# GpSimd's product of a decode chunk one half step after VectorE's join, and the transposes of a three-tile block one step on

## The chip, the cores and the metric

One core of a Trainium2 chip runs the kernel. The time is the device time of one execution in microseconds (us); three runs of the kernel before gave 1037.73 us in the median (1034.54 to 1038.38). TensorE multiplies, VectorE (DVE), ScalarE (ACT) and GpSimd (POOL) do the elementwise work, SyncE (SP) issues most DMAs. Each engine works through its own queue in order.

## The reference, cut to what matters

```python
# attention over packed keys, 4 x 8 heads, 576 tokens, head_dim 64  -> x, 2304 x 512
logits = x @ w_gate + log1p(exp(x @ w_noise)) * noise          # 8 experts
top2   = the two largest of 8, weights by softmax
for e in range(8):                                             # expert layer
    h = maximum(x[mask_e] @ w1[e], 0)                          # 512 -> 1024
    out[mask_e] += weight * (h @ w2[e])                        # 1024 -> 512
g = x @ w_gate2; val = x @ w_val                               # gated layer, 512 -> 1536
return (silu(g) * val) @ w_out                                 # 1536 -> 512
```

The three matrices of the gated layer come in as 64-bit numbers (`wx`), so the kernel has to turn them into pairs of 32-bit parts before it can multiply with them. That is the decode.

## The kernel before

Every product in full precision is made of three matmuls, high by high, high by low and low by high (`mm3`, L628 to L630), in which a value is split into a rounded part and its remainder. The program has three stretches: attention and routing (to about 160 us), the expert layer (to about 605 us) and the gated layer (to the end). The change lies in the expert layer.

**The expert steps.** The expert layer runs over 14 blocks. A block is one expert with three tiles of 128 tokens, or with two: (0,·,3), (1,·,3), then a three-tile and a two-tile block for each of the experts 2 to 5, then (6,·,3), (7,·,3), (6,·,2), (7,·,2). A block has eight steps f = 0 to 7. TensorE does in step f: the up product of f (L628 to L630 on `xTh`, `xTl`), the down product of f - 1 (on `hh`, `hl`), and transposes for the next block where there are any. ScalarE makes `hh` from the up product (L664), VectorE makes `hl` (L665). So `hh` of step f is needed one step later. With three tiles the down products hold three of the eight PSUM banks for the whole block; the up product, the transposes and the decode take turns in the other five.

**What else is issued in a step, in this order.** First `loader.turn()`: it copies a piece of the next expert's weights from `stg` (ACT L148), subtracts for the remainder (L149; on VectorE for a piece of w1, on GpSimd for a piece of w2), and SP issues the load of a later piece (L142). A turn falls in steps 1, 3, 5, 7 of most blocks, but in all eight of the block of expert 1. Then `prep`: one step of `prep_expert` for the next block. Its first steps gather a row tile each (GpSimd's indirect DMA, L623), its later ones transpose a tile each (PE L610, ACT L611, DVE L612). The list `PREP` says in which f the generator takes a step; for a next block of three tiles these are six, three gathers and three transposes. Last the decode: two half steps in a step of a three-tile block (none in f = 0 from expert 2 on), one in a step of a two-tile block.

**The decode.** There are 72 chunks of 128 x 256 numbers. Chunk m is loaded (SP, L763, tile `wd`), masked into exponent and mantissa (`exps`, DVE L771 and L772, tiles `ex` and `mt`), made to floats in a PSUM bank (`floats`, ACT L778 and L779), joined (DVE L785 and L787, which frees the bank), and multiplied on GpSimd (L795). For an odd chunk of the first two matrices GpSimd then makes four sums and differences (L801), and for every odd chunk ScalarE makes the high part (`high`, L818), VectorE the low part (`low`, L824), and SP stores it (`store`, L829). Counted in half steps of the generator, chunk m has its load in 2m, `exps` in 2m + 4, `floats` in 2m + 7, join and product in 2m + 9, `high` in 2m + 11, `low` in 2m + 12 and `store` in 2m + 13. `wd` has five buffers, `ex` and `mt` three each, a pair's `sums` two. The generator has 156 half steps; the blocks up to the last one take exactly 156, and the last block first runs the generator to its end (L1170), before it closes the decode's buffers and opens those of the gated layer's weights in their place.

Of the kernel before, what the change touches and what calls it, by code (L numbers as in the profile page):

```python
# [11 lines left out]
F32 = mybir.dt.float32  # L12
# [3 lines left out]
I32 = mybir.dt.int32  # L16
# [83 lines left out]
def body(ctx, tc, qT, kT, v, pT, noise, wgn, w1, w2, wx, out):  # L100
# [31 lines left out]
    def bank():  # L132
        return psum.tile([128, 512], F32, name="bank", tag="bank")
# [610 lines left out]
    for x in PLAN.split():  # L744
        x, _, n = x.partition("*")
# [4 lines left out]
    dp = wB[2]  # L750
# [5 lines left out]
    def decode():  # L756

        st, sums, his = {}, {}, {}

        def load(n):  # L760
            i, c = divmod(n, 4)
            w = dp.tile([128, 256, 2], I32, name="wd", bufs=5)
            nc.sync.dma_start(w, wx[i, :, c * 256:(c + 1) * 256].bitcast(I32).rearrange("p (n two) -> p n two", two=2))  # L763
            st[n] = [w]

        def exps(n):
            w = st[n][0]
            ex = dp.tile([128, 256], I32, name="ex")
            mt = dp.tile([128, 256], I32, name="mt")
            st[n] += [ex, mt]  # L770
            ve.tensor_scalar(ex, w[:, :, 1], 0x7FF00000, None, op0=ALU.bitwise_and)  # L771
            ve.tensor_scalar(mt, w[:, :, 1], 0xFFFFF, None, op0=ALU.bitwise_and)  # L772

        def floats(n):
            w, ex, mt = st[n]
            fl = bank()
            st[n].append(fl)
            nc.scalar.activation(fl[:, :256].bitcast(I32), ex, AF.Relu, bias=nb896, scale=8.0)  # L778
            nc.scalar.activation(fl[:, 256:], mt, AF.Copy, bias=1.0, scale=2.0 ** -20)  # L779

        def join(n):
            w, ex, mt, fl = st.pop(n)
            i, c = divmod(n, 4)
            mf = mt.bitcast(F32)
            ve.scalar_tensor_tensor(ex, w[:, :, 1], -(1 << 31), fl[:, :256].bitcast(I32), op0=ALU.bitwise_and,  # L785
                                    op1=ALU.bitwise_or)
            ve.scalar_tensor_tensor(mf, w[:, :, 0].bitcast(U32), 2.0 ** -52, fl[:, 256:], op0=ALU.mult, op1=ALU.add)  # L787
            if c % 2 == 0:
                sums[i, c // 2] = dp.tile([128, 8, 128], F32, name="sums", bufs=2)
            q = sums[i, c // 2]  # L790
            if i % 3 == 2:
                o = q[:, 2 * (c % 2):2 * (c % 2) + 2]
            else:
                o = q[:, 4:7:2] if c % 2 else q[:, 0::7]
            nc.gpsimd.tensor_tensor(o, mf.rearrange("p (f n) -> p f n", f=2),  # L795
                                    ex.bitcast(F32).rearrange("p (f n) -> p f n", f=2), op=ALU.mult)
            if c % 2 and i % 3 < 2:

                for o, x, y, op in ((2, 7, 6, ALU.add), (3, 0, 7, ALU.subtract), (1, 2, 0, ALU.subtract),
                                    (5, 4, 1, ALU.subtract)):  # L800
                    nc.gpsimd.tensor_tensor(q[:, o], q[:, x], q[:, y], op=op)  # L801

        def place(n, x):
            i, c = divmod(n, 4)
            p, m = divmod(i, 3)
            o = wq[2 * p + m][:, x, c // 2] if m < 2 else wxo[p][:, x, c // 2 * 512:c // 2 * 512 + 512]
            return o.bitcast(F32)

        def pair(n):

            i, c = divmod(n, 4)
            return sums[i, c // 2], 7 if i % 3 < 2 else 4

        def high(n):
            if n % 2:
                q, k = pair(n)
                h = his[n] = dp.tile([128, 7, 128], F32R, name="his", bufs=1)
                nc.scalar.copy(h[:, :k], q[:, :k])  # L818
                nc.scalar.dma_start(place(n, 0), h[:, :k].bitcast(F32).rearrange("p s n -> p (s n)"))

        def low(n):
            if n % 2:
                q, k = pair(n)
                ve.tensor_tensor(q[:, :k], q[:, :k], his.pop(n)[:, :k].bitcast(F32), op=ALU.subtract)  # L824

        def store(n):
            if n % 2:
                q, k = pair(n)
                nc.sync.dma_start(place(n, 1), q[:, :k].rearrange("p s n -> p (s n)"))  # L829

        N = 72
        for n in range(N + 6):
            for half in (((0, load), (2, exps), (6, low)), ((4, join), (6, store), (5, high), (3, floats))):
                for d, fn in half:
                    if 0 <= n - d < N:
                        fn(n - d)
                yield
# [307 lines left out]
    def xp_acc(i):  # L1145
# [8 lines left out]
    PREP = {2: [1, 0, 1, 0, 0, 1, 1, 0], 3: [1, 1, 1, 1, 1, 1, 0, 0]}  # L1154
    prep0 = prep_pair(0, slot0, FIRST_PLAN)

    blocks = [(0, 2, 3), (1, 2, 3)] + [b for e in range(2, E - 2) for b in ((e, 0, 3), (e, 3, 2))]
    blocks += [(E - 2, 0, 3), (E - 1, 0, 3), (E - 2, 3, 2), (E - 1, 3, 2)]
    dec_g = decode()
    stream = Stream()  # L1160
    rws = ExitStack()
    for i, blk in enumerate(blocks):
# [11 lines left out]
        for f in range(8):  # L1174
# [5 lines left out]
            if f in {4: (1, 2, 4, 5, 7), 3: (0, 1, 2, 3)}.get(left, range(8) if e == 1 else (1, 3, 5, 7)):  # L1180
                loader.turn()
            if [1, 1, 0, 0, 1, 1, 0, 0][f] if left == 2 else PREP[blocks[i + 1][2]][f] if left > 1 else 0:
                next(prep, None)
# [171 lines left out]
```

## Time and profile before

| | |
|---|---|
| median of three runs | 1037.73 us |
| the profiled execution | 1037.31 us |
| its span, first to last instruction | 1035.5 us |
| mean granted clock of TensorE | 0.982 |
| busy: PE, DVE, ACT, POOL | 978.0, 678.6, 421.5, 355.5 us |

A span is the time between the first and the last instruction of the program; the time of the run lies 1.8 us above it. A wait in the profile is the idle time of an engine ahead of an instruction, put down to what ended it. The granted clock is 1.00 where TensorE ran at 2.4 GHz and 0.5 where it ran at 1.2 GHz, averaged over a stretch.

### The profile page before, as it was taken

The numbers are of one execution on the slowest core, as the hardware profiler recorded it, in microseconds if no ns is written. First come the engines' busy times: TensorE is split into PE (matmuls) and PEld (weight loads), VectorE is DVE, ScalarE is ACT, GpSimd is POOL, SyncE is SP. The second block draws the span as 40 slices with busy tenths as digits, with TensorE's granted clock in tenths as the row PEclk, the third lists the DMA queues.
The fourth block names the chain that finished last, engine by engine and source line by source line (L and its number), as shares of the span: only waits on it lengthen the run. The fifth ranks groups of instructions, "written<-read, shape, count | busy, mean of one in ns | idle before, by whom it ended". The sixth has DMA issues, their size and how long they took to land.

```text
span 1035.5 us, 15235 instructions
## 1 busy us (share of the span) xinstructions
PE 978.0 (94%) x5415; PEld 864.9 (84%) x5415; DVE 678.6 (66%) x1536; ACT 421.5 (41%) x859; POOL 355.5 (34%) x409
## 2 busy tenths in 40 slices
PE   6967799989999899998999999999999999999996
PEld 3534689979888798998988898999999999999995
DVE  5998973466565646555645475678865678756764
ACT  2665253465455545555544434222423224132220
POOL 1333532344643545445454414321232211111100
PEclk9978999999999999999999999999999999999999
DMA  8934543377675767666764679887798768777741
GB/s 288 299 122 146 170 136 116 126 273 269 212 264 191 270 204 251 229 202 245 246 225 159 194 210 311 238 236 214 217 303 235 230 184 255 234 199 222 216 147 65
DMA packets 99045, 221.41 MB, mean 214 GB/s; under 512 B 8080, under 2 KB 37392, under 8 KB 96656
## 3 DMA queue, kind: packets, MB, share of 16 engines
q0 software_dynamic: 46752, 104.87, 34.9%
q1 hardware_dynamic: 47024, 101.32, 28.9%
q10 hardware_dynamic: 5184, 14.16, 3.6%
q8 instruction: 45, 0.74, 0.3%
q14 instruction: 40, 0.33, 0.1%
HBM read 172.08 MB, written 48.23 MB: 213 GB/s over the span
## 4 chain that ended last, share of the span: by engine, by line
PE 74%; DVE 10%; DMA 5%; POOL 3%; issue 3%; ACT 3%; SPq 0%; ACTq 0%; POOLq 0%; DVEq 0%
PE bank L628 23%; PE bank L630 23%; PE bank L629 23%; DMA row<-x_dram,idx 3%; POOL sums L801 1%; DMA stg<-in_w 1%; PE bank L610 1%; PE bank L388 1%; POOL w L149 1%; DVE p L460 1%; DVE sums L824 1%; PE bank L919 1%; ACT w L148 1%; POOL sums L795 1%; DMA kt<-in_kT 1%
## 5 line engine op out<-in xcount | busy, mean ns | idle before, releaser
L628 PE MATMUL bank<-w 128*128 128x384 f32 x504 | 170.4, 338 | 0.6 <-ACT hh L993 0.5
L630 PE MATMUL bank<-w 128*128 128x384 f32 x504 | 168.7, 335 | 0.0
L629 PE MATMUL bank<-w 128*128 128x384 f32 x504 | 168.6, 334 | 0.0
L628 PE MATMUL bank<-xTh,w 128*128 128x256 f32 (+1 forms) x512 | 163.1, 319 | 2.8 <-DVE mt L787 2.8
L630 PE MATMUL bank<-xTh,w 128*128 128x256 f32 (+1 forms) x512 | 159.9, 312 | 0.0
L629 PE MATMUL bank<-xTl,w 128*128 128x256 f32 (+1 forms) x512 | 159.7, 312 | 0.0
L665 DVE SCALAR_TENSOR_TENSOR hl<-bank,hh 128x384 fp32r<-128x384 f32 (+1 forms) x128 | 62.4, 488 | 132.3 <-ACT hh L664 125.8
L871 POOL DMA_DIRECT2D w<-wq x72 | 54.4, 756 | 266.3 <-PE bank L630 266.3
L628 PE MATMUL bank<-w,hh 128*128 128x512 f32 x320 | 127.0, 397 | 6.1 <-ACT hh L664 6.1
L630 PE MATMUL bank<-w,hl 128*128 128x512 f32 x320 | 127.4, 398 | 2.8 <-DVE hl L665 2.8
L629 PE MATMUL bank<-w,hh 128*128 128x512 f32 x320 | 127.1, 397 | 0.0
L795 POOL TENSOR_TENSOR sums<-mt,ex 128x256 f32<-128x256 f32 x72 | 54.4, 755 | 170.4 <-DVE mt L787 163.8
L149 POOL TENSOR_TENSOR w<-stg,w 128x1024 fp32r<-128x1024 f32 x37 | 91.4, 2475 | 62.3 <-ACT w L148 62.0
L628 PEld LDWEIGHTS bank<-xTh,w 128*128 128x128 f32 x512 | 98.2, 192 | 7.8 <-DVE mt L787 3.5
L629 PEld LDWEIGHTS bank<-xTl,w 128*128 128x128 f32 x512 | 98.3, 192 | 3.5
L664 ACT ACTIVATE hh<-bank 128x384 fp32r<-128x384 f32 (+1 forms) x128 | 55.5, 433 | 111.5 <-PE bank L630 103.1
L630 PEld LDWEIGHTS bank<-xTh,w 128*128 128x128 f32 x512 | 98.2, 192 | 0.0
L628 PEld LDWEIGHTS bank<-w 128*128 128x128 f32 x504 | 94.6, 188 | 3.1 <-ACT hh L993 1.1
L629 PEld LDWEIGHTS bank<-w 128*128 128x128 f32 x504 | 94.7, 188 | 0.7
L630 PEld LDWEIGHTS bank<-w 128*128 128x128 f32 x504 | 94.6, 188 | 0.0
L630 PE MATMUL bank<-w,lg 128*128 128x512 f32 x204 | 79.7, 391 | 0.0
L629 PE MATMUL bank<-w,hg 128*128 128x512 f32 x204 | 79.7, 390 | 0.0
(222 smaller groups left out, 1838.4 us busy)
## 6 DMA issues: line engine op xcount, KB each, us to landing
w<-wq POOLq DMA_DIRECT2D x36, 1024.0 KB
stg<-in_w SPq DMA_DIRECT2D x64, 512.0 KB
w<-wq POOLq DMA_DIRECT2D x36, 768.0 KB
wd<-in_wx SPq DMA_DIRECT2D x72, 256.0 KB
w<-wxo POOLq DMA_DIRECT2D x18, 1024.0 KB
wq<-his ACTq DMA_DIRECT2D x24, 448.0 KB
wq<-sums SPq DMA_DIRECT2D x24, 448.0 KB
y_dram<-row SPq DMA_DIRECT2D x40, 256.0 KB
```

The source lines that it names most:

```text
L148: nc.scalar.copy(hi, st)
L149: lo_eng.tensor_tensor(lo, st, hi.bitcast(F32), op=ALU.subtract)
L388: nc.tensor.matmul(PS["o", t, c][:n, :272], E2T[t][:, c * 128:c * 128 + n], PP[t], start=True, stop=True)
L460: el.scalar_tensor_tensor(p, p, c[k], x, op0=ALU.add, op1=ALU.mult)
L610: nc.tensor.transpose(ps[:, k, :n], src[:n, k * 128:(k + 1) * 128], ident[:n, :n])
L628: nc.tensor.matmul(ps, lh, rh, start=start, stop=False, skip_group_check=skip)
L629: nc.tensor.matmul(ps, lh, rl, start=False, stop=False, skip_group_check=skip)
L630: nc.tensor.matmul(ps, ll, rh, start=False, stop=stop, skip_group_check=skip)
L664: nc.scalar.activation(hh[:, :n], ps[:, :n], AF.Relu)
L665: ve.scalar_tensor_tensor(hl[:, :n], ps[:, :n], 0.0, hh[:, :n].bitcast(F32), op0=ALU.max, op1=ALU.subtract)
L795: nc.gpsimd.tensor_tensor(o, mf.rearrange("p (f n) -> p f n", f=2), ex.bitcast(F32).rearrange("p (f n) -> p f n", f=2), op=ALU.mult)
L871: nc.gpsimd.dma_start(w[:, :4 * m].rearrange("p (x n) -> p x n", x=4), src.rearrange("p h k n -> p (h k) n"))
```

## The change

The product and GpSimd's sums leave `join` and become a function of their own, `times`, which is issued in the half step after the join. `high`, `low` and `store` move on by one half step each, the load by one half step too, and the order within the half steps changes: the first half step of a round now issues `times`, `exps`, `store`, `high`, the second one `join`, `load`, `low`, `floats`. Chunk m then has its load in 2m + 1, `exps` in 2m + 4, `floats` in 2m + 7, the join in 2m + 9, the product in 2m + 10, `high` in 2m + 12, `low` in 2m + 13, `store` in 2m + 14. The generator has 158 half steps. `wd` has four buffers, `ex` and `mt` four each, which is the same memory. Apart from that, the transposes for a next block of three tiles are made in the steps 4, 5, 6 instead of 3, 4, 5; its gathers stay in 0, 1, 2.

```diff
-            w = dp.tile([128, 256, 2], I32, name="wd", bufs=5)
+            w = dp.tile([128, 256, 2], I32, name="wd", bufs=4)
...
-            ex = dp.tile([128, 256], I32, name="ex")
-            mt = dp.tile([128, 256], I32, name="mt")
+            ex = dp.tile([128, 256], I32, name="ex", bufs=4)
+            mt = dp.tile([128, 256], I32, name="mt", bufs=4)
...
         def join(n):
-            w, ex, mt, fl = st.pop(n)
-            i, c = divmod(n, 4)
+            w, ex, mt, fl = st[n]
             mf = mt.bitcast(F32)
             ve.scalar_tensor_tensor(ex, w[:, :, 1], -(1 << 31), fl[:, :256].bitcast(I32), op0=ALU.bitwise_and,
                                     op1=ALU.bitwise_or)
             ve.scalar_tensor_tensor(mf, w[:, :, 0].bitcast(U32), 2.0 ** -52, fl[:, 256:], op0=ALU.mult, op1=ALU.add)
+
+        def times(n):
+            w, ex, mt, fl = st.pop(n)
+            i, c = divmod(n, 4)
+            mf = mt.bitcast(F32)
             if c % 2 == 0:
                 sums[i, c // 2] = dp.tile([128, 8, 128], F32, name="sums", bufs=2)
...
-        for n in range(N + 6):
-            for half in (((0, load), (2, exps), (6, low)), ((4, join), (6, store), (5, high), (3, floats))):
+        for n in range(N + 7):
+            for half in (((5, times), (2, exps), (7, store), (6, high)), ((4, join), (0, load), (6, low), (3, floats))):
...
-    PREP = {2: [1, 0, 1, 0, 0, 1, 1, 0], 3: [1, 1, 1, 1, 1, 1, 0, 0]}
+    PREP = {2: [1, 0, 1, 0, 0, 1, 1, 0], 3: [1, 1, 1, 0, 1, 1, 1, 0]}
```

## Rows read from the trace of the kernel before

**Rows 1.** The page: the chain that ended last, shares by engine.
```profile
PE 74%; DVE 10%; DMA 5%; POOL 3%; issue 3%; ACT 3%; SPq 0%; ACTq 0%; POOLq 0%; DVEq 0%
```
**Rows 2.** Windows of the expert layer: length, busy (count) by engine, clock, DMA.
```profile
205.00:620.00 415.00, 397.62 (x2220) 356.89 (x2219) 241.56 (x510) 208.62 (x391) 196.85 (x227) 0.99 0.67 228
...
220.00:240.00 20.00, 17.59 (x84) 15.96 (x83) 15.45 (x29) 11.19 (x19) 9.49 (x10) 0.91 0.75 258
```
**Rows 3.** Waits from 205 to 620 us: waiter <- releaser: total us, times, longest.
```profile
POOL sums L795 <- DVE mt L787: 133.2, 41, 6.5
...
ACT his L818 <- POOL sums L801: 31.3, 13, 4.9
...
ACT w L148 <- DMA stg<-in_w: 21.9, 12, 4.5
...
DVE ex L771 <- POOL sums L795: 12.8, 9, 2.9
...
PE bank L610 <- DMA row<-x_dram,idx: 8.3, 4, 2.8
...
PE bank L628 <- ACT hh L664: 6.1, 6, 2.5
...
PE bank L628 <- DVE mt L787: 2.8, 2, 2.4
...
DVE ex L771 <- DMA wd<-in_wx: 2.5, 1, 2.5
```
**Rows 4.** Timeline (start, us, engine, line): first up matmuls of neighbouring steps.
```profile
233.04 0.33 PE L628 MATMUL bank<-xTh,w 128*128 128x384 f32 x1
...
237.23 0.33 PE L628 MATMUL bank<-xTh,w 128*128 128x384 f32 x1
...
278.83 0.28 PE L628 MATMUL bank<-xTh,w 128*128 128x256 f32 x1
...
281.64 0.28 PE L628 MATMUL bank<-xTh,w 128*128 128x256 f32 x1
```
**Rows 5.** Timeline of POOL in the two-tile block of expert 2.
```profile
271.89 2.81 POOL L801 TENSOR_TENSOR sums<-sums 128x128 f32<-128x128 f32 x4
...
279.33 3.00 POOL L149 TENSOR_TENSOR w<-stg,w 128x1024 fp32r<-128x1024 f32 x1 [2.80 <-ACT w L148]
```
**Rows 6.** Timeline of POOL in the two-tile block of expert 3.
```profile
337.86 0.74 POOL L795 TENSOR_TENSOR sums<-mt,ex 128x256 f32<-128x256 f32 x1 [5.93 <-DVE mt L787]
338.68 1.95 POOL L801 TENSOR_TENSOR sums<-sums 128x128 f32<-128x128 f32 x4
340.84 0.98 POOL L623 DMA_INDIRECT row<-x_dram,idx  x1 [0.22 <-PE bank L630]
...
344.43 0.96 POOL L623 DMA_INDIRECT row<-x_dram,idx  x1 [0.16 <-issue]
```
**Rows 7.** Timeline of PE in the same block: transposes that waited.
```profile
347.81 0.63 PE L610 MATMUL bank<-ident,row 128*128 128x128 f32 x4 [2.81 <-DMA row<-x_dram,idx]
```
**Rows 8.** Timeline of ACT ahead of the two-tile block of expert 2.
```profile
274.73 0.94 ACT L818 CAST his<-sums 128x896 fp32r<-128x896 f32 x1 [3.60 <-POOL sums L801]
...
276.91 0.37 ACT L664 ACTIVATE hh<-bank 128x256 fp32r<-128x256 f32 x1
```
**Rows 9.** Timeline of DVE: `low` and then the join, in expert 1's block.
```profile
220.82 1.08 DVE L824 TENSOR_TENSOR sums<-sums,his 128x896 f32<-128x896 f32 x1
...
222.15 0.41 DVE L787 SCALAR_TENSOR_TENSOR mt<-wd,bank 128x256 f32<-128x256 uint32 x1
```
**Rows 10.** Timeline of DVE: a `low` beside POOL's L149 of rows 5.
```profile
278.98 1.08 DVE L824 TENSOR_TENSOR sums<-sums,his 128x896 f32<-128x896 f32 x1
```
**Rows 11.** The page's groups: POOL's subtraction, busy, mean ns of one, idle before.
```profile
L149 POOL TENSOR_TENSOR w<-stg,w 128x1024 fp32r<-128x1024 f32 x37 | 91.4, 2475 | 62.3 <-ACT w L148 62.0 <-issue 0.2
```
**Rows 12.** Waits of SP's queue from 200 to 600 us.
```profile
SPq L763 <- DVE mt L787: 76.7, 30, 6.6
```

## The prediction

> **What bounds the kernel now.** I read the shares of the chain that ended last first: TensorE holds 74% of it [rows 1], so only what makes TensorE wait is worth anything. Then the stretch that the change touches. From 205 to 620 us TensorE is busy for 397.62 of 415 us, so it idles 17.4 us [rows 2]; all 17.4 is the most that shorter waits can give back, but for the clock. The granted clock is 0.91 in two windows of 20 us there, the one shown and the one from 460 us, and 1.00 in the others [rows 2]: 0.09 x 20 = 1.8 us lost in each, both times right behind a long wait. The ceiling is 17.4 + 3.6 = 21.0 us. The waits view says which instructions end the idle time: transposes wait 8.3 us in four places for gathered rows, down products 6.1 us in six places for ScalarE's `hh`, up products 2.8 us in two for a bank that the join frees [rows 3]. Last the timelines around these, for what stood ahead in each queue. A step takes 237.23 - 233.04 = 4.19 us with three tiles and 281.64 - 278.83 = 2.81 us with two [rows 4]; these are the units in which the change moves work.
>
> **Part 1, the transposes.** All four waits for rows lie in the two-tile blocks of experts 2 to 5, where the three-tile block of the next expert is prepared. Expert 3's shows the longest: the first gather starts at 340.84 and its transposes at 347.81, 6.97 us later and after a wait of 2.81 [rows 6, 7]; the other three are of this kind and no longer [rows 3]. One step on is 2.81 us too, so with the gathers where they are now the late tile is in time, by a hair. The next tile decides. In expert 3's block TensorE would have reached its transposes at 347.81 - 2.81 = 345.0; two steps and one set of transposes (some 0.45 us) later, at 351.1, it comes to the second tile, whose gather starts at 344.43 [rows 6] and lands by 344.43 + 6.97 = 351.4. That is 0.3 us late at worst.
>
> The gathers also start earlier. In f = 0 the program issues the gather ahead of the decode. Today the product of the half step before stands in front of it on GpSimd, waiting 5.93 us for the join, and its sums take until 340.6 [rows 6]. With the change that product is behind the gather. The gather of f = 1 gains little: product, sums and a subtraction of 2.48 us still stand ahead of it. I leave 1.0 us of these waits standing, and count the clock dip behind the longest one as gone: 8.3 + 1.8 - 1.0 = **9.1 us**. Bounds: 4.5 us, if the gathers start half a two-tile step (1.4 us) later than now, and 10.1 us.
>
> What the move costs: the third tile is transposed in f = 6, with one step instead of two before the next block's first up product. Its copies need about 0.6 and 0.7 us, the rest of f = 7 covers them. No up product waits for `xTl` on the matmul queue today [rows 3]. I take 0; without the cover it is rival C.
>
> **Part 2, the product.** GpSimd waits 133.2 us for joins, ScalarE's `high` waits 31.3 us in 13 places for GpSimd's sums, and VectorE's masks 12.8 us in nine for products that still read `ex` [rows 3]. These waits are coupled: ScalarE's `high` is held for 3.60 us, until GpSimd's last sum at 274.7, and the `hh` behind it comes two us later, for which TensorE then waits [rows 5, 8]. After the change `high` stands one half step later, which in a three-tile block is a whole step of 4.19 us, while the product can still run right after its join. 13 waits of 31.3 / 13 = 2.4 us, 4.9 at most, mostly end. The fourth buffer of `ex` and `mt` gives the masks two half steps behind the product instead of one: the 12.8 us go as well, though VectorE has room and I count them 0.
>
> What is late next: where GpSimd's subtraction of a weight piece comes in the same step as an odd chunk's product, the product now stands behind it, and the subtraction waits for ScalarE's copy. Counted through the loops, this coincidence occurs in nine steps before and in six after, and three of the six are in expert 1's block, where a turn falls in every step and ScalarE's copies wait for the loads (part of the 21.9 us in rows 3). There subtraction, product and sums take 2.48 + 0.75 + 2.0 = 5.2 us after the copy [rows 6, 11], 1.0 us more than the step that `high` was given.
>
> In expert 1's block the join also moves ahead of `low`. Today `low` runs from 220.82 and the join ends at 222.56 [rows 9]; TensorE's longest wait for a bank ends there. That bank is free up to 1.08 us sooner, but the first transposes still take a bank that leaves the up product behind them with the last join's, so the wait shrinks and does not end. Waits for `hh` and banks with the second dip are 6.1 + 2.8 + 1.8 = 10.7 us. About 4.9 of it lie in expert 1's block (the 2.4, the dip, and one short `hh` wait); I keep 3.0 there. Of the other 5.8 I keep 1.8, for expert 7's block, where ScalarE waits up to 4.5 us for a load of weights [rows 3] whatever GpSimd does. That recovers 10.7 - 4.8 = **5.9 us**. Bounds: -6 us (the product behind subtractions and gathers in all six steps, 1.0 us each) and 10.7.
>
> One row speaks against half of it: a subtraction on GpSimd beside a `low` took 3.00 us, where the mean is 2.475 [rows 5, 10, 11]: `low` ended at 280.06, 0.73 us after that subtraction began. `low` now follows the join directly, so it meets the product which the join releases, for each of the 36 odd chunks. The Trainium skill, SBUF — State Buffer, section "SBUF: two separate sides", says that VectorE and GpSimd share a pair of ports as an exclusive lock, held for a whole instruction. The trace agrees, by these 0.5 us. By that rule the product starts up to 1.08 us after the join, takes back what the reordering gave it, and the forecast would be about 1 us longer.
>
> **Part 3, loads, buffers, tail.** The load comes a half step later and waits for the join of its own half step, as a fifth buffer is gone. SP already waits 76.7 us for joins here [rows 12]. Masks wait for a chunk's arrival once today, 2.5 us [rows 3]; a half step less is 2.81 us in a two-tile block, VectorE can hide that up to once a step, so the load costs between 0 and a few us. I take 0; what stands behind it on SP is rival D. The two extra half steps fall ahead of the last block and hold only the last `store`. If the gathers and loads that reuse the decode's buffers wait for it, this costs up to one step, 2.8 us; I take 0, since VectorE's `low` before it has only moved by one step. New waits that I can't place (0 to 5 us) I set against the intervals between matmuls that are too short for the waits view and shrink with the rest (some 3 us).
>
> **The sum.** 9.1 + 5.9 = 15.0 us, taken from the profiled execution's 1037.31 us (0.4 us under the median of the runs shown): 1022.3, so **1022 us**. Its own range, with 5 us for the new waits and 5 for what I left standing, is 1017 to 1027.
>
> **The rivals.**
> A, the forecast: 58%.
> B, only the transposes gain. The product's waits move into the queue behind subtractions and come back as `hh` waits. For it: the idle time of rows 11 ahead of the subtraction, 62 us on ScalarE's copies. Against it: in two-tile blocks the new order has no such coincidence at all. 1037.3 - 9.1 = 1028, 17%.
> C, given back at block starts. Seven blocks are prepared with the third tile in f = 6; if ScalarE's queue, with a copy of 1 us and `high` of 0.94 us in front, brings `xTl` 2 us late, that is 7 x 2 = 14 us back and the time 1036. Against it: in f = 6 there is mostly no turn, where f = 5 had one. 14%.
> D, slower: SP is held by the joins, so pieces of weights are loaded later. Twelve copies on ScalarE wait for their load already, 21.9 us together [rows 3]. Later by one two-tile step each they would hold `hh` for 12 x 2.8 = 33.6 us more, and the time is 1037.3 - 15 + 33.6 = 1056. It decides above 15 / 12 = 1.3 us a piece. Against it: SP's loads stand behind `low` or a join now, and the join will come before `low`. 11%.
> That the change does nothing can't be: the instructions move in the queues. It could be nothing to TensorE, which is C's time.
>
> **How the numbers follow.** 0.5% (5.2 us) is about what can be told from no change: below 1032.5 is faster, above 1042.9 slower. Faster: A, B and a part of C, 58 + 17 + 4 = 79%. Same: 8 of C and 4 of D, 12%. Slower: 7 of D and 2 of C, 9%. The range reaches down to the ceiling, 1037.3 - 21 = 1016, less 2 us for the short intervals, and up past B to the first of C's cases, 1034.
>
> **What would show it.** Right: no transposes waiting for `row<-x_dram`; `high` waiting under 10 us for sums; PE idle in the expert layer under 8 us; the clock at 1.00 from 460 to 480 us. Wrong: up products that wait for `xTl` at a block's start (C), or more than 30 us of ScalarE's copies waiting for `stg` (D). If `hh` waits stay at 6 us with the product now behind L149, B holds.

## The result, and the profile after

The changed kernel takes 1019.97 us in the median of six runs (1017.95 to 1023.58), the kernel before beside it 1037.84 (1034.54 to 1042.45, six runs). The ratio is 0.9831 (95% interval 0.9803 to 0.986); a second set, beside other runs of the kernel before, gave 0.9827 (0.9803 to 0.985). Forecast were 1022 us and a range of 1014 to 1034. The profiled execution took 1019.91 us, its span is 1018.0: 17.4 us of time and 17.5 of span less than before.

The chain that ended last in the changed kernel, shares by engine, against [rows 1]:

```profile
PE 78%; DVE 11%; DMA 5%; ACT 2%; issue 2%; POOL 1%; SPq 0%; ACTq 0%; DVEq 0%; POOLq 0%
```

Windows, columns as in [rows 2], first the one from 460 us in the kernel before, then the changed kernel; the two of 20 us had a clock of 0.91 before:

```profile
460.00:480.00 20.00, 17.29 (x106) 15.50 (x105) 9.82 (x23) 9.94 (x17) 12.61 (x15) 0.91 0.71 251
```

```profile
205.00:620.00 415.00, 410.31 (x2315) 371.33 (x2314) 270.43 (x531) 217.66 (x409) 229.87 (x238) 1.00 0.74 244
220.00:240.00 20.00, 18.04 (x93) 16.15 (x94) 16.27 (x27) 12.77 (x24) 11.28 (x10) 1.00 0.79 247
460.00:480.00 20.00, 20.00 (x121) 18.34 (x120) 12.41 (x27) 10.20 (x19) 13.36 (x13) 1.00 0.66 226
```

TensorE idles 4.7 us of the 415 (17.4 before). Waits of the changed kernel over the same stretch, to be read against [rows 3]:

```profile
POOL sums L799 <- DVE mt L786: 28.3, 18, 3.4
ACT w L148 <- DMA stg<-in_w: 27.6, 16, 3.8
...
ACT his L822 <- POOL sums L805: 2.8, 2, 1.7
PE bank L628 <- DVE mt L786: 2.8, 2, 1.6
...
PE bank L630 <- DVE hl L665: 0.9, 1, 0.9
...
PE bank L628 <- ACT hh L664: 0.7, 1, 0.7
...
DVE ex L771 <- POOL sums L799: 0.2, 1, 0.2
```

No transposes wait for rows (8.3 us before). ScalarE's `high` waits 2.8 us for sums (31.3), GpSimd 28.3 us for joins (133.2), the masks 0.2 us for products (12.8). Nearly all that is left of TensorE's waits, 4.3 of 4.7 us, stands in one place, the block of expert 1 and the first steps behind it. TensorE's timeline of the changed kernel shows these four:

```profile
212.67 0.50 PE L630 MATMUL bank<-w,hl 128*128 128x512 f32 x1 [0.91 <-DVE hl L665]
220.74 0.45 PE L628 MATMUL bank<-xTh,w 128*128 128x384 f32 x1 [1.57 <-DVE mt L786]
226.85 0.44 PE L628 MATMUL bank<-xTh,w 128*128 128x384 f32 x1 [1.21 <-DVE mt L786]
242.86 0.50 PE L628 MATMUL bank<-w,hh 128*128 128x512 f32 x1 [0.65 <-ACT hh L664]
```

To see where the time came from I cut the span at the first up matmuls of three steps: f = 0 of expert 1's block, f = 2 of the block behind it, f = 6 of the last block. The starts lie at 196.86, 245.60 and 601.53 us before, at 196.47, 245.17 and 582.56 us after. So the ten steps around expert 1's block took 48.74 us and now take 48.70. **Nothing was gained there.** The 92 steps of the experts 2 to 7 took 355.93 and now take 337.39: 18.5 us gained. From the last cut to the span's end it is 433.97 before and 435.44 after, 1.5 us more. That can't be put down to the change: over the fourteen profiles this length goes from 433.8 to 436.3, with 433.8 in a kernel that has most of the change and 435.1 in one that has none of it. Two of the cuts, in the kernel before and in the changed one, then the stretch of the 92 steps in both, by the windows view:

```profile
245.60 0.33 PE L628 MATMUL bank<-xTh,w 128*128 128x384 f32 x1
...
601.53 0.28 PE L628 MATMUL bank<-xTh,w 128*128 128x256 f32 x1
```

```profile
245.17 0.34 PE L628 MATMUL bank<-xTh,w 128*128 128x384 f32 x1
...
582.56 0.28 PE L628 MATMUL bank<-xTh,w 128*128 128x256 f32 x1
```

```profile
245.60:601.53 355.93, 341.67 (x1931) 306.24 (x1929) 199.12 (x434) 178.25 (x339) 173.10 (x202) 1.00 0.66 224
```

```profile
245.17:582.56 337.39, 337.31 (x1930) 305.66 (x1929) 213.36 (x436) 178.30 (x338) 194.17 (x203) 1.00 0.71 239
```

For each experiment these two lengths are in this table, each from one profiled execution (two of the changed kernel agree within 0.3 us):

| kernel | ratio to before, 95% | expert 1, ten steps | experts 2 to 7 |
|---|---|---|---|
| before | 1 | 48.74 | 355.93 |
| changed | 0.9831 (0.9803–0.986) | 48.70 | 337.39 |
| changed, second time | 0.9827 (0.9803–0.985) | 48.76 | 337.10 |
| transposes alone | 0.994 (0.992–0.996) | 50.30 | 353.82 |
| decode alone | 0.9906 (0.9882–0.993) | 50.33 | 349.25 |
| product moved, `high` not | 1.0146 (1.0123–1.0169) | 56.11 | 365.17 |
| `high` moved, product not | 0.9875 (0.9846–0.9903) | 51.04 | 343.32 |
| `low` ahead of the join | 0.9893 (0.9865–0.992) | 50.49 | 341.68 |
| transposes two steps on | 1.0 (0.9984–1.0016) | 54.73 | 350.36 |
| expert 2's remainders on VectorE | 0.9786 (0.9753–0.9819) | 48.80 | 338.26 |
| loads spread | 0.9765 (0.9742–0.9787) | 43.13 | 337.09 |
| loads spread, `high` moved, product not | 0.9796 (0.9754–0.9839) | 43.13 | 338.93 |
| loads spread, `low` ahead of the join | 0.9836 (0.98–0.9873) | 43.13 | 342.60 |
| loads spread in the kernel before | 1.0018 (0.9996–1.0041) | 48.57 | 358.97 |

The kernel before ran at 1036.8 to 1040.6 us beside these in the median, so the ratios are what compares.

### The profile page after: what moved, and what is told of

The parts are those of the page before. It is cut to its first block, busy times and chain, and to the rows that moved or that the text cites. A ratio compares the mean times of both kernels' runs of the same rounds, so it can differ in the third digit from the quotient of the medians.

```text
span 1018.0 us, 15328 instructions
## 1 busy us (share of the span) xinstructions
PE 972.8 (96%) x5415; PEld 863.0 (85%) x5415; DVE 695.8 (68%) x1536; ACT 421.2 (41%) x859; POOL 378.7 (37%) x409
## 4 chain that ended last, share of the span: by engine, by line
PE 78%; DVE 11%; DMA 5%; ACT 2%; issue 2%; POOL 1%; SPq 0%; ACTq 0%; DVEq 0%; POOLq 0%
PE bank L628 24%; PE bank L630 24%; PE bank L629 24%; DMA stg<-in_w 1%; PE bank L610 1%; PE bank L388 1%; DVE p L460 1%; DMA out<-row 1%; DMA y_dram<-row 1%; DMA kt<-in_kT 1%; PE bank L263 1%; PE bank L923 1%; POOL w L149 0%; DVE ohr L561 0%; DVE ohc L563 0%
## 5 line engine op out<-in xcount | busy, mean ns | idle before, releaser
L149 POOL TENSOR_TENSOR w<-stg,w 128x1024 fp32r<-128x1024 f32 x37 | 90.4, 2448 | 95.3 <-ACT w L148 95.2
L799 POOL TENSOR_TENSOR sums<-mt,ex 128x256 f32<-128x256 f32 x72 | 72.9, 1014 | 92.1 <-DVE mt L786 55.8
```

What stands on the lines that cost most here:

```text
L149: lo_eng.tensor_tensor(lo, st, hi.bitcast(F32), op=ALU.subtract)
```

## The experiments

**Each part alone.** The kernel before with the new `PREP`, and the changed kernel with the old one:

```diff
-    PREP = {..., 3: [1, 1, 1, 1, 1, 1, 0, 0]}
+    PREP = {..., 3: [1, 1, 1, 0, 1, 1, 1, 0]}
```

> Only PREP is changed, the decode is as before. The theory (two causes that add: late rows, and a product that holds ScalarE) expects the four waits for gathered rows gone, 8.3 us and the clock dip from 460 to 480 us, and the rest as before: hh and bank waits of 9 us, ScalarE's high still waiting some 31 us for sums; time about 1028. Rival 'the decode is all, the gathers are only late because the product stands ahead of them': the rows stay late by a step and wait on; 1034 to 1038.

> The decode as changed, the transposes in f = 3, 4, 5 as before. The theory expects hh and bank waits as after the change (some 4 us, in expert 1's block), high's wait under 10 us; gathers start as after the change, so the second tile of the four two-tile blocks is late by 1.2 to 1.4 us each (gather at 338.4 in expert 3's block, lands some 6.9 us later, TensorE comes at 344.1): 5 us of waits for rows; time about 1025. Rival 'the decode is all': no waits for rows, 1020. Rival 'the transposes are all': 8 us of waits for rows and 1035.

The transposes alone take 0.6% off (0.4 to 0.8), about 6.2 us; the decode alone 0.94% (0.7 to 1.18), about 9.8 us. Together 16.0, near the 17.9 of the whole; each is less than I had expected of it (1028 and 1025 us, measured 1033.9 and 1030.9 beside a kernel before at 1040.1). Waits from 205 to 605 us with the transposes alone:

```profile
ACT his L818 <- POOL sums L801: 33.6, 13, 4.9
...
PE bank L628 <- ACT hh L664: 9.5, 8, 3.1
PE bank L630 <- DVE hl L665: 3.9, 4, 1.9
PE bank L628 <- DVE mt L787: 2.7, 2, 1.8
```

The rows are in time, with the gathers where they were (340.67 us in expert 3's block), but `hh` and `hl` are waited for 13.4 us where it was 6.3. Of this 2.8 us stand one step behind the four places where transposes had waited: as TensorE no longer stops for rows, it runs into the split of the up product. The other new waits stand in expert 1's block (2.3 us) and behind 520 us (2.1). That `high` holds the split up on ScalarE fits its 33.6 us of waits for sums, but is not shown for each place. (This profile is of an execution at 1037.32 us, among the two longest of eight, so its waits overstate.) With the decode alone the rows stay late, 6.4 us where it was 8.3, as the gathers start earlier (the first one in expert 3's block at 332.59):

```profile
PE bank L610 <- DMA row<-x_dram,idx: 6.4, 4, 1.9
PE bank L628 <- ACT hh L664: 4.1, 3, 2.5
PE bank L628 <- DVE mt L786: 2.2, 3, 1.2
```

**Which move in the decode carries it.** The changed kernel with `high`, `low` and `store` back in their old half steps, then with the product back beside the join:

```diff
-(((5, times), (2, exps), (7, store), (6, high)), ((4, join), (0, load), (6, low), (3, floats)))
+(((5, times), (2, exps), (6, low)), ((4, join), (0, load), (6, store), (5, high), (3, floats)))  # product only
+(((2, exps), (7, store), (6, high)), ((4, join), (4, times), (0, load), (6, low), (3, floats)))  # high only
```

> Changed kernel, but high, low and store stay in the half steps that they had before (2m + 11, 2m + 12, 2m + 13); only the product moves (2m + 10). Theory: what ends the hh waits is that high stands a step further behind the product, not that the product moves in GpSimd's queue. So high waits again, 30 us or more (the product now sometimes behind a subtraction as well), hh waits 5 to 8 us, gathers on time: about 1027. Rival 'the product's place in the queue is what counts': high waits under 10 us, 1020.

> Changed kernel, but the product stays in the join's half step (2m + 9); high, low and store are as in the changed kernel (2m + 12 to 2m + 14). Theory: hh waits are gone outside expert 1's block, high's wait under 10 us; the gathers stand behind the product again and start up to 3 us later in f = 0, which the shifted transposes still cover: 1020 to 1022. Expert 1's block may even be better, as the product is not behind a subtraction. Rival 'the product's place is what counts': 1026 to 1030.

The product's move without `high`'s makes the kernel slower than it was before, by 1.46% (1.23 to 1.69); I had expected it faster, at 1027 us. Counted in half steps, `high` stands two behind the product in the kernel before and in the changed one, one in this kernel, three in the one with `high` moved alone. Waits of that kernel, then its longest stop, in the timelines of GpSimd, ScalarE and TensorE:

```profile
ACT his L822 <- POOL sums L805: 62.9, 21, 6.7
...
PE bank L628 <- ACT hh L664: 18.2, 13, 4.9
```

```profile
541.51 2.38 POOL L149 TENSOR_TENSOR w<-stg,w 128x1024 fp32r<-128x1024 f32 x1 [9.99 <-ACT w L148]
...
547.60 1.81 POOL L805 TENSOR_TENSOR sums<-sums 128x128 f32<-128x128 f32 x4
...
549.44 0.94 ACT L822 CAST his<-sums 128x896 fp32r<-128x896 f32 x1 [5.87 <-POOL sums L805]
...
551.61 0.47 ACT L664 ACTIVATE hh<-bank 128x384 fp32r<-128x384 f32 x1
...
552.14 0.79 PE L628 MATMUL bank<-w,hh 128*128 128x512 f32 x1 [4.87 <-ACT hh L664]
```

Read from the top: the subtraction waits for ScalarE's copy, the product and the sums stand behind it, `high` waits 5.87 us for them at the head of ScalarE's queue, `hh` waits behind `high`, TensorE waits 4.87 us for `hh`. With `high` moved and the product not, `high` waits 0.9 us once, and the ratio is 0.9875. Both kernels have the new `PREP`, which gives 0.994 alone, and the changed buffers and place of the load, which no run takes out. So the later `high` is the move that gains without the other; the product's move costs 2% against the transposes alone and adds some 0.4% behind the later `high`, with intervals that overlap. I had expected 1020 to 1022 us of `high` alone and it is 1028. GpSimd's product waits 61.4 us for its join there, against 28.3 in the changed kernel, but these waits alone don't set the price: the same order has 64.4 us of them with the loads spread (below), and TensorE then waits 1.0 us in the experts 2 to 7, where it waits 4.6 us without the spread.

**The order of `low` and join.**

```diff
-((4, join), (0, load), (6, low), (3, floats))
+((6, low), (4, join), (0, load), (3, floats))
```

> The changed kernel with `low` ahead of the join again. Theory 1 (the product now meets `low` on a shared port, and the join is what frees a bank): the product's mean falls from 1.01 us to about 0.8 us, the product starts sooner after its join, but the three short waits for a bank in expert 1's block grow by up to 1.1 us each, and joins in the other blocks free their bank 1.1 us later; the time is 2 to 5 us above the changed kernel's (ratio 0.985 to 0.988). Theory 2 (the bank has room outside expert 1's block, and the order of the two on VectorE does not matter to TensorE): within 1 us of the changed kernel's time. Theory 3 (the port's loss weighs more): 1 to 2 us below it.

The direction is theory 1's, the size is more than it had (0.9893 against 0.985 to 0.988): 0.66% above the changed kernel beside it, 6.8 us by the ratios. The product's mean does fall, from 1.03 to 0.87 us. The place is wider than expected: the experts 2 to 7 lose 4.6 us against the changed kernel beside it, expert 1's block 1.7. In that block TensorE waits 3.96 us in one piece for a bank, and the window from 220 us is back at a clock of 0.91.

**One step of cover for the last tile.**

```diff
-    PREP = {..., 3: [1, 1, 1, 0, 1, 1, 1, 0]}
+    PREP = {..., 3: [1, 1, 1, 0, 0, 1, 1, 1]}
```

> The changed kernel with the transposes for a three-tile block in the steps 5, 6, 7 instead of 4, 5, 6. Theory 1 (the third tile needs f = 7 as its cover, as the prediction took it; without it rival C holds): the copies of 0.6 us on ScalarE and 0.7 us on VectorE come between the last transposes and the next block's first up product, some 1.6 us at each of seven block starts, 11 us in all, with new rows of the matmul queue waiting for `xTh` or `xTl`; the time is about 1031 (ratio 0.993). Theory 2 (the matmuls already queued hide the copies): no such rows, the time within 1.5 us of the changed kernel's.

The whole gain is gone, ratio 1.0, more than the 11 us expected. At each of the seven block starts the first up product now waits for its own copies; the timeline of TensorE shows one of them, the waits view six:

```profile
481.87 0.60 PE L610 MATMUL bank<-ident,row 128*128 128x128 f32 x4
...
483.27 0.44 PE L628 MATMUL bank<-xTh,w 128*128 128x384 f32 x1 [0.81 <-ACT xTh L611]
...
484.65 0.44 PE L629 MATMUL bank<-xTl,w 128*128 128x384 f32 x1 [0.94 <-DVE xTl L612]
```

```profile
PE bank L628 <- ACT xTh L611: 5.4, 6, 1.9
...
PE bank L629 <- DVE xTl L612: 3.9, 6, 0.9
```

That is 9.3 us in such rows; the seventh start lies ahead of 205 us, with 1.0 us more. The loss is 18 us by the ratios, by the table 6.0 in the ten steps around expert 1's block and 13.3 in the experts 2 to 7. Of these 13.3 TensorE's idle time makes 8.0, by the windows of that stretch, and the clock from 480 us 1.8; the other 3.5 lie in its busy time.

**What is left in expert 1's block.** Two attempts. One takes GpSimd's subtractions out of that block, the other spreads the weights of expert 2 over the blocks of experts 0 and 1, with a turn in every other step:

```diff
-            loader = Loader(expert_pieces(e + 1, (ve, nc.gpsimd)) ...)
+            loader = Loader(expert_pieces(e + 1, (ve, ve if e == 1 else nc.gpsimd)) ...)   # on VectorE
...
-        if (t0 == 0 and e < E - 1) or e == 1:
+        if (t0 == 0 and e < E - 1) or i == 0:                                             # spread
...
-            loader = Loader(expert_pieces(e + 1, (ve, nc.gpsimd)) if e + 1 < E else ())
+            loader = Loader(expert_pieces(max(e + 1, 2), (ve, nc.gpsimd)))
...
-            if f in {4: ..., 3: ...}.get(left, range(8) if e == 1 else (1, 3, 5, 7)):
+            if f in {4: ..., 3: ...}.get(left, (1, 3, 5, 7)):
```

> The changed kernel with all remainders of expert 2's weights made on VectorE in expert 1's block, so that GpSimd has no subtraction there; the turns still fall in all eight steps. Theory 1 (the prediction's: what is left there comes from GpSimd's subtraction, product and sums in one step, which hold ScalarE's `high`): `high` waits nowhere over 0.5 us in that block, the masks are not held beside a subtraction, TensorE's 3.7 us of waits there fall under 1 us, and the time is 3 to 5 us below the changed kernel's (ratio 0.979). Theory 2 (the weights' loads come too late when a turn falls in every step, and ScalarE's copy, VectorE's subtraction and the join stand behind them): ScalarE still waits up to 3.5 us for `stg`, TensorE's waits there stay at 3 us or more, and VectorE's subtraction of 1.2 us in every step makes the time the same or up to 5 us longer (ratio 0.983 to 0.988).

> The changed kernel with the pieces of expert 2's weights spread over the blocks of experts 0 and 1, a turn in every other step, where the block of expert 1 had a turn in all eight. Theory 1 (what is left of TensorE's waits, 4.3 us in four places, comes from the turn that falls in every step of expert 1's block, where GpSimd's subtraction, product and sums come in one step): these waits fall under 1 us, ScalarE's `high` waits nowhere over 0.5 us there, and the time is 3 to 5 us below the changed kernel's (ratio 0.979). Theory 2 (the waits come from the banks, which the decode's two half steps fill, whatever the weights do): the waits stay at 3 us or more and the time within 1 us. Theory 3 (the block of expert 0 has no room for the turns): waits of the same size appear there and the time is the same or some us above.

Without subtractions on GpSimd `high` waits 0.5 us in all, and the block takes 48.80 us as before. Its ratio, 0.9786, has an interval that overlaps the changed kernel's. The timelines of ScalarE, VectorE and TensorE in this kernel say why nothing moved in the block:

```profile
216.40 1.05 ACT L148 CAST w<-stg 128x1024 fp32r<-128x1024 f32 x1 [4.08 <-DMA stg<-in_w]
...
217.48 1.22 DVE L149 TENSOR_TENSOR w<-stg,w 128x1024 fp32r<-128x1024 f32 x1 [2.27 <-ACT w L148]
...
219.91 0.41 DVE L786 SCALAR_TENSOR_TENSOR mt<-wd,bank 128x256 f32<-128x256 uint32 x1
...
220.37 0.44 PE L628 MATMUL bank<-xTh,w 128*128 128x384 f32 x1 [1.86 <-DVE mt L786]
```

The load comes late, ScalarE's copy waits 4.08 us for it, VectorE's subtraction waits for the copy, masks and join stand behind the subtraction, and the bank that the join frees is what TensorE waits for. As VectorE's subtraction now stands ahead of the join, the run shows that the block is as long without the coincidence on GpSimd, not that the coincidence was free. With the loads spread, the ten steps take 43.13 us, 5.6 less. Windows of this kernel:

```profile
205.00:605.00 400.00, 399.21 (x2269) 362.96 (x2268) 258.98 (x518) 208.14 (x394) 226.88 (x236) 1.00 0.71 240
220.00:240.00 20.00, 20.00 (x106) 18.03 (x105) 13.29 (x27) 11.38 (x22) 9.81 (x8) 1.00 0.58 205
```

TensorE is busy 399.21 of 400 us: the expert layer now stands on its matmuls. This is the fastest version, 1012.83 us in the median (1012.6 to 1014.3), ratio 0.9765.

**What needs the spread, and what it needs.** The same spread with the product back beside the join, in the kernel before, and with `low` first:

```diff
-        if (t0 == 0 and e < E - 1) or e == 1:
+        if (t0 == 0 and e < E - 1) or i == 0:
...
```

> The loads of expert 2 spread as before, all else as in the changed kernel, but the product back in the join's half step (only `high`, `low` and `store` a half step later). Theory 1 (the product's own move is worth something in every block, since a product that stands waiting for its join holds GpSimd's gathers and subtractions): the waits for `hh` that this order had outside expert 1's block, three of 1.3 to 2.1 us, stay; the time is 4 to 6 us above the one with the product moved (ratio 0.981). Theory 2 (the product's move was only worth something in expert 1's block, where a turn fell in every step): no wait over 0.6 us in the expert layer, the ratio 0.9765 as with the product moved.

> The kernel before, with expert 2's weights spread over the blocks of experts 0 and 1 and nothing of the change. Theory 1 (the spread ends what expert 1's block costs and touches nothing else): the 2.4 and 0.7 us of waits there and the clock's dip between 220 and 240 us go, 4.9 us, and the time is about 1033 on this count (ratio 0.995); the waits for rows in the two-tile blocks stay at 8 us. Theory 2 (a wait removed in one block lets the next come up, as with the transposes alone): under 2 us gained, ratio above 0.998.

> The loads of expert 2 spread, with `low` ahead of the join. Theory 1 (the order of `low` and join decides only in expert 1's block, where banks are short): nothing of the 5.7 us that this order cost without the spread is left, no wait for a bank over 0.6 us, ratio 0.976 to 0.978. Theory 2 (a join 1.1 us later delays `hl` and banks in every block): waits for `hl` of 0.6 to 1.3 us, as there were two from 460 us on, and the time 2 to 4 us above the one with the join first (ratio 0.979 to 0.981).

In the kernel before, the spread gains nothing (1.0018, 0.9996 to 1.0041), though ScalarE waits less for loads (0.6 us in the ten steps where it was 8.7): there `high` holds ScalarE, 6.12 us for sums ahead of 214.04, and TensorE still waits 1.9 us for the bank (2.4 before). The two causes stand in series, and either alone keeps the block at 48.6 to 48.7 us. The spread itself does two things, which no run separates: the loads come earlier, and five pieces are copied in these ten steps instead of eight. With the product beside the join the spread gives 0.9796; its interval overlaps 0.9765, so what the product's move is still worth there, 1.8 us by the table, isn't settled by the times. What TensorE waits for in that kernel is rows, 1.0 us in two places. With `low` first the loss is back (0.9836), all of it in the experts 2 to 7, 5.5 us; no wait for a bank shows, but one of 1.26 us for `hl` and a window at 0.91 behind it. By these rows the bank was not the reason outside expert 1's block: `low` waits for ScalarE's `high` (7.9 us in four places there, 4.6 in three with the join first), and with `low` first the join and `hl` stand behind that wait in VectorE's queue. No run takes this wait away alone.

## Why the prediction was right, and where by luck

The total missed by 2 us and the mechanism held: the waits for rows and most of those for `hh` are gone. The parts were off in ways that in part cancelled, and that is luck. In the experts 2 to 7 the change gave 18.5 us where the prediction's terms come to 13.1 (9.1 and 5.8 less 1.8); expert 1's block gave nothing where they had 1.9; ahead of the first cut 0.4 came, behind the last one 1.5 went, neither shown to be the change's.

- **The ceiling.** 17.4 us of waits and 3.6 of clock were read right. What came out of the experts 2 to 7 is 18.5 us, of which 14.2 are idle time, all of it in the waits listed there before, 1.8 the window from 460 us, and 2.6 busy time: TensorE is busy 341.67 us before and 337.31 after in the same steps, and the clock explains 1.8 of these 4.4. The prediction had "some 3 us" for intervals too short for the waits view and set them against new waits. The size fits, the place doesn't: the windows show no idle time beyond the listed waits. No new waits came in the experts 2 to 7. So the 5.4 us above the 13.1 are these 2.6, the 1.0 kept for rows and the 1.8 kept for expert 7's block.
- **Part 1, 9.1 us.** The rows are in time in all four blocks. In expert 3's two-tile block, which starts at 329.29 us now and at 332.38 before, the first gather starts at 328.95 where it was 340.84 ([rows 6]): 12 us earlier in a kernel that is 3 us ahead there. The second tile, which the prediction took to decide, is gathered at 338.37 where it was 344.43, 3 us earlier beside the block's start. So the margin was no hair. The product that waited for its join ahead of the first gather is behind it now. The 1.0 us kept was not needed: even without the earlier gathers, with the transposes alone, no row is waited for. But as a gain the transposes were worth 6.2 us alone (4.2 to 8.3): of the waits removed, 2.8 us came back one step later as waits for `hh` and `hl`. GpSimd's timeline of the changed kernel, the first two gathers:

```profile
328.95 1.99 POOL L623 DMA_INDIRECT row<-x_dram,idx  x1
...
338.37 1.07 POOL L623 DMA_INDIRECT row<-x_dram,idx  x1
```

- **Part 2, 5.9 us.** Undersized: 9.8 us alone (7.3 to 12.3), though 1.9 us less of waits for rows (8.3 to 6.4) are in it, which the prediction counted in part 1. The step named as its cause, the later `high`, is the one that carries it, and the runs with one move each show it. But its distance from the product stays at two half steps; what grew is the distance from the join. The prediction spoke of the product as free to run right after its join, while the change issues it a half step later; that this move alone would cost 2%, some 21 us against the transposes alone, it did not see.
- **Expert 1's block.** The failed step. The prediction took 1.9 of 4.9 us away there and kept 3.0 for GpSimd's subtraction, product and sums in one step. Nothing was gained: 3.1 us of waits and the clock's dip went, waits of 0.91, 1.57, 1.21 and 0.65 us came. The coincidence is there (`high` waits 1.71 us for sums at 219.18), but without it the block is as long. What holds the block is the turn in every step with its late loads: spread, they give back 5.6 us. The prediction had this in rival D, as a danger of the change; it was a cost of the kernel before, hidden behind `high`. Counted from the block's first matmul, ScalarE's eight copies start within 1.1 us of where they did before; it now waits for the load where it waited for sums.
- **Expert 7's block.** 1.8 us were kept for its wait for a load. None was left: 480 to 605 us show TensorE busy 124.92 of 125.
- **Part 3.** Loads, buffers and masks cost nothing that TensorE sees in the experts 2 to 7. ScalarE waits 27.6 us for `stg`, 21.9 before: D's sign, under its 30 us. The growth stands in the ten steps around expert 1's block (14.1 us, 8.7 before), which gained nothing; what of it is the later load of the decode no run separates.
- **The rivals.** B falls, as `hh` is waited for 0.7 us. C did not come, but its mechanism is real: one step later the same tile takes the whole gain back. The step of cover in f = 7 that the prediction counted on is what separates 0.983 from 1.0.

## What to carry to other kernels

Where an in-order queue is held by an instruction that waits for another engine, move that consumer later before you move its producer: moved apart, each beside transposes that alone give 0.994, they gave 0.9875 and 1.0146. A view of waits shows only the last cause of a stop; before pricing what will be left, ask what else is late at that point, since causes in series give nothing until the last is gone. And price a wait above its idle time: in the experts 2 to 7 a wait took some 0.2 to 0.3 us more from TensorE than the view lists (2.6 us over 11 waits in the kernel before, 3.5 over 12 with the transposes two steps on). The length of a stretch from one matmul to another, compared between kernels, shows at once where a gain came from and when a stretch has reached its matmuls.

## What the hardware showed that was not expected

VectorE and GpSimd slow each other more than [rows 5] had shown, and VectorE suffers too. GpSimd's product takes 1014 ns in the mean and 755 before, VectorE's `low` 1192 and 950, by the groups of the profile. For `low` it decides which of the two started first: in the changed kernel, on 128x896, it took 1.08 to 1.09 us in all 14 places where GpSimd's arithmetic began during it, and 1.58 to 3.33 us in the six where a subtraction of GpSimd was already running. Two places in the timelines of the changed kernel, a mask beside a subtraction and a product beside a `low`:

```profile
222.85 2.41 POOL L149 TENSOR_TENSOR w<-stg,w 128x1024 fp32r<-128x1024 f32 x1 [2.97 <-ACT w L148]
...
223.89 1.51 DVE L771 TENSOR_SCALAR ex<-wd 128x256 int32<-128x256 int32 x1
```

```profile
331.07 1.09 DVE L828 TENSOR_TENSOR sums<-sums,his 128x896 f32<-128x896 f32 x1
...
331.24 1.52 POOL L799 TENSOR_TENSOR sums<-mt,ex 128x256 f32<-128x256 f32 x1 [0.30 <-DVE mt L786]
```

The mask ends at 225.40, 0.14 us after the subtraction; the product at 332.76, 0.60 after `low`, where a product alone takes 0.75. Over the changed kernel's rows, masks (L771) that overlap no GpSimd arithmetic take 285 ns in the mean (34 of them), the others 568 (38, up to 2004). The joins (L784), which read a PSUM bank, take 412 and 410. The Trainium skill, SBUF — State Buffer, section "SBUF: two separate sides", names as takers of the shared pair of ports a VectorE operation in a two-port mode or with two SBUF inputs; this agrees with `low`, which has two SBUF inputs, being held, and with the joins, which have one, being spared. The masks have one too, so by that list they would have to run in a two-port mode, which no run shows. What this costs TensorE stays open: the two masks ahead of the wait of 1.21 us at 226.85 took 2.3 us together instead of 0.6, but no run took this away alone.
